# A scan beside a fused feed-forward: one y visit per chunk, and one scan operation between w and gT of each step

## The chip, the cores and the metric

The kernel runs on one core of a Trainium2 chip. The metric is the device time of one execution in microseconds (us); lower is better. All data are fp32.

## The reference

A Mamba-2 scan (4 sequences, 8 heads, 768 positions, head dimension 32, state dimension 16) is followed by a feed-forward block with the gate h cos h. In chunks, with `L` the running products of the decays `a`:

```python
M = CB * L                                  # CB = C B^T inside a chunk, causal
y_intra = M @ x
y_inter = (C @ state) * decay_to_i
y = y_intra + y_inter
state = decay_full * state + sum_j(B x * decay_from_j)
...
h = x @ w_in                                # x: y as 3072 rows of 256
g = h * cos(h)
out = g @ w_out                             # 256 -> 2048 -> 256
```

## The kernel before

The scan goes in 6 chunks (c = 0 to 5) of 128 positions. The feed-forward of one chunk, 4 x 128 = 512 rows, takes 16 *steps* (NF = 16), so there are 96 steps n. All engines follow one order written out by hand: the loop over n at the end. The scan of chunk c (c >= 1) is put into the steps of chunk c-1 and, before the change, the first steps of its own; chunk 0's scan stands ahead of the loop. "Place p of a chunk" is step 16(c-1) + p, for the scan of chunk c.

One step n issues, in this order:

- `first(n)`: TensorE computes hp = w_in^T y for 256 of the features and half of the rows (4 matmuls, 8 records, L512). ScalarE rounds it to k (L516), VectorE forms w = hp/2pi - k (L518).
- `gate(n)`: ScalarE takes the sine in place (L523). In steps 0 to 14 a `join` may follow, which assembles fp32 weights from their parts (VectorE L207 and L209, POOL L217).
- `gated(n)`: VectorE forms gT = hp * w (L528). From step 16 on, `differ(n)` follows on POOL: three products in a row that form gd from gT (L553, L555, L556).
- `second(n - 2)`: TensorE adds into o with gT and gd of two steps earlier. For chunk 0 that is 4 matmuls (L571); for the others `seven`, a scheme of 7 products (14 records, L609), in the order 1, 2, 6, 7, 5, 4, 3. Products 1 and 2 need gT, product 6 needs L555's output, product 7 is the first into the upper of o's two PSUM banks. After each eighth step the sums come out: ps is copied by ScalarE (L618) and VectorE (L619), then POOL makes four sums (L624), then DMAs on the SP queue. That is issued at steps 9 and 1 of a chunk's 16 (n = 25, 33, 41, ...). `differ_w`, two POOL products at a time (L547), stands in steps 14, 15, 17 and 19.

The scan of a chunk has these parts:

- `decays` (halves): VectorE's running product lam, 128 x 512, two for each sequence b (L344). After the second half, POOL forms sc (`weigh`, L327), and SP gets the load of that sequence's row `arow` for the next chunk.
- `reaches`: two running products of 128 for a pair of sequences u (L335); after them SP gets the load `along`.
- `turn2` (tp, L405): four transposes, copies bT and cT on ScalarE, rT on VectorE (L413).
- `intra2` (g, L422) one step later, and `masked`: m = g * lam, two VectorE operations per sequence (L435), the pair's first sequence in the g step, its second one a step later.
- `finish2` three steps after turn2: y of the pair, from the carried state (L447, tiles of 32 x 64 of the array) and from m (L454, tiles of 128 x 32), copied to yT by ScalarE (L459); then the chunk's sums s_ps (L471) and `carry`, two VectorE `whole` operations (L487) and a POOL product (L491).

For pair 0 of chunk c turn2 stands at place 11, for pair 1 at place 19 (`TURN`); the halves stand in the four steps ahead of each (chunk 1's first pair: steps 4, 6, 8, 9). In a step, masked, finish2, halves and reaches come after `second`.

PSUM has two hp buffers, so hp of step n+2 waits until gT of step n has read its own; two o banks; and two pair buffers ("scan") that tp, g, y and s_ps take in turn. m has two buffers.

Of the kernel before, what the change touches and what calls it, by code (L numbers as in the profile page):

```python
# [8 lines left out]
FP32 = mybir.dt.float32  # L9
# [16 lines left out]
def kernel(  # L26
# [62 lines left out]
    def pair(name):  # L89

        return psum.tile([P, 2, 4 * P], FP32, tag="scan", bufs=2, name=name)
# [109 lines left out]
    def join(which, i):  # L201

        parts = held.pop((which, i), ())
        for e, (high, bits, last) in enumerate(parts):
            V.tensor_scalar(out=bits, in0=bits, scalar1=3, scalar2=0x3FFFFFFF,  # L207
                            op0=ALU.logical_shift_left, op1=ALU.bitwise_and)
            V.scalar_tensor_tensor(out=bits, in0=high, scalar=0xC0000000, in1=bits,  # L209
                                   op0=ALU.bitwise_and, op1=ALU.bitwise_or)  # L210
            dst = kept(which, i)
            if len(parts) > 1:
                dst = dst[:, :, e * P:(e + 1) * P]
            else:
                bits, last = (ap.rearrange("p (k f) -> p k f", k=dst.shape[1])
                              for ap in (bits, last))
            G.tensor_tensor(out=dst.bitcast(U32), in0=bits, in1=last, op=ALU.add)  # L217
# [16 lines left out]
    unit = const.tile([P, HH, P], FP32, name="unit")  # L234
    G.tensor_copy(out=unit, in_=ident.unsqueeze(1).to_broadcast([P, HH, P]))

    unit0 = const.tile([P, H, W], FP32, name="unit0")
    for t in range(2):
        ts = slice(t * W, (t + 1) * W)
        V.tensor_copy(out=unit0[ts], in_=ident[ts, ts].unsqueeze(1).to_broadcast([W, H, W]))  # L240
# [30 lines left out]
                    axis=mybir.AxisListType.XY, op=ALU.add)  # L271


    a0s = const.tile([P, 2, H, W], FP32, name="a0s")
    halves = a0z.rearrange("p (t i) -> p t i", t=2)
    for h in range(HH):
        ACT.activation(a0s[:, :, h], halves, AF.Copy, scale=mine[:, h:h + 1])
    for t in range(2):
        G.tensor_tensor(out=a0s[:, t, HH:H], in0=halves[:, t:t + 1].to_broadcast([P, HH, W]),
                        in1=mine[:, HH:H].unsqueeze(2).to_broadcast([P, HH, W]), op=ALU.mult)  # L280
    tos = const.tile([P, H, W], FP32, name="tos")
    G.tensor_tensor(out=tos, in0=to.unsqueeze(1).to_broadcast([P, H, W]),
                    in1=mine.unsqueeze(2).to_broadcast([P, H, W]), op=ALU.mult)

# [83 lines left out]
    def intra(b):  # L368
        bT, cT = part[0, b]
        g = [pair("g") for _ in range(2)]  # L370
        for q in range(4):
            r = slice(32 * q, 32 * q + 32)
            PE.matmul(g[q // 2][:, q % 2, 0:2 * P], lhsT=bT[r],
                      rhs=cT[r].rearrange("p t (s i) -> p s t i", s=2), start=True, stop=True)
        l = lam.pop((0, b))
        m = scan.tile([P, 2, H, W], FP32, tag="m", name="m")
        for q in range(2):
            of = [t[:, :, q * HH:(q + 1) * HH].rearrange("p s (k t) i -> p k s (t i)", k=2)
                  for t in (m, l)]
            V.tensor_tensor(out=of[0], in0=g[q][:, :, 0:2 * P].rearrange(  # L380
                "p k (s i) -> p k s i", s=2), in1=of[1], op=ALU.mult)
        part[0, b] = m
# [16 lines left out]
    def turn2(c, u):  # L399
        bc = raw[c][0]  # L400

        tp = pair("tp")[:, 0].rearrange("p (s k i) -> p s k i", s=2, k=2)
        for s in range(2):
            for k in range(2):
                PE.transpose(tp[:, s, k],  # L405
                             bc[:, k, heads(2 * u + s)].rearrange("p h n -> p (h n)"), ident)
        bT = scan.tile([P, 2, P], FP32, tag="bT2", bufs=1, name="bT2")
        ACT.copy(out=bT, in_=tp[:, :, 0])
        cT = scan.tile([P, 2, 2, P], FP32, tag="cT2", bufs=1, name="cT2")
        for t in range(2):  # L410
            ACT.activation(cT[:, :, t], tp[:, :, 1], AF.Copy, scale=slot[:, t:t + 1])
        rT = scan.tile([P, 2, P], FP32, tag="rT", bufs=1, name="rT")
        V.tensor_tensor(out=rT, in0=tp[:, :, 1], in1=reach[c, u], op=ALU.mult)  # L413
        part[c, u] = [bT, cT, rT]

# [10 lines left out]
    def masked(c, b):  # L426

        u, s = divmod(b, 2)
        g, ms = part[c, u][0:2]
        l = lam.pop((c, b))  # L430
        m = scan.tile([P, H, P], FP32, tag="m", name="m")
        for q in range(2):
            of = [t[:, q * HH:(q + 1) * HH].rearrange("p (k t) i -> p k (t i)", k=2)
                  for t in (m, l)]
            V.tensor_tensor(out=of[0], in0=g[q][:, :, s * 2 * P:(s + 1) * 2 * P], in1=of[1],  # L435
                            op=ALU.mult)
        ms.append(m)

    def finish2(c, u):
        (_, ms, rT), xr = part.pop((c, u)), raw[c][1]  # L440
        y = pair("y")


        for s in range(2):
            for q in range(4):
                r, p = slice(32 * q, 32 * q + 32), 64 * (q % 2)
                PE.matmul(y[p:p + 64, q // 2, s * P:(s + 1) * P],  # L447
                          lhsT=state[c - 1, u][r, s].rearrange("p t d -> p (t d)"),
                          rhs=rT[r, s], start=(s == 0), stop=False, tile_position=(32 * q, p),
                          skip_group_check=True)  # L450
        for s in range(2):
            for h in range(H):
                q, t = h % 4, h // 4
                PE.matmul(y[32 * q:32 * q + 32, t, s * P:(s + 1) * P], lhsT=xr[:, 2 * u + s, h],  # L454
                          rhs=ms[s][:, h], start=False, stop=True, tile_position=(0, 32 * q),
                          skip_group_check=True)
        if u == 0:
            yT[c] = two.tile([P, 2, TB], FP32, tag="yT", name="yT")
        ACT.copy(out=yT[c][:, :, 2 * u * P:(2 * u + 2) * P], in_=y[:, :, 0:2 * P])  # L459
        if c < NC - 1:  # L460
            s_ps = pair("s_ps")[:, 0, 0:4 * D].rearrange("p (s d) -> p s d", s=2)
            for s in range(2):
                sum_up(c, 2 * u + s, s_ps[:, s])
            carry(c, u, s_ps)

    def sum_up(c, b, s_ps):

        xr, sc = raw[c][1], scaled.pop((c, b))
        for q in range(4):
            two_ = slice(2 * q, 2 * q + 2)  # L470
            PE.matmul(s_ps[32 * q:32 * q + 32], lhsT=sc[:, two_].rearrange("p h n -> p (h n)"),  # L471
                      rhs=xr[:, b, two_].rearrange("p h d -> p (h d)"), start=True, stop=True,
                      tile_position=(0, 32 * q), skip_group_check=True)
# [210 lines left out]
    for dst, src in ((a_cut, cut), (a_all, la)):  # L684
# [13 lines left out]
                 NF + 1: [(0, hind), (1, hind)], NF + 3: [(2, hind), (3, hind)]}  # L698


    TURN = (NF - 5, NF + 3)

    halves_of = {u: [(t - 4 + i, 2 * u + i // 2, i % 2) for i in range(4)]
                 for u, t in enumerate(TURN)}
    ahead = {1: {0: [(4, 0, 0), (6, 0, 1), (8, 1, 0), (9, 1, 1)]}}

    sums = {}

# [18 lines left out]

    def pairs(n):

        at = [(1 + (n - t) // NF, u) for u, t in enumerate(TURN) if (n - t) % NF == 0]  # L730
        return [(c, u) for c, u in at if 0 < c < NC]

    def halves_at(n):
        return [(c, b, t) for c in range(1, NC) for u in range(2)
                for m, b, t in ahead.get(c, {}).get(u, halves_of[u]) if m + (c - 1) * NF == n]

    EARLY = 3
    rest_of_loads()
    for n in range(NC * NF + LAG):
        c, f = divmod(n, NF)  # L740
        early = n < EARLY
        if n < NC * NF:
            if f == 0 and c > 0:
                load(c + 2)
            first(n)
            if n == 0:
                first_scan()
            for at in pairs(n):
                turn2(*at)
            rests = [grade(*piece[m], later=True)  # L750
                     for m in ((n,) if early else ()) + ((n + 1,) if n >= EARLY - 1 else ())
                     if m in piece]
            gate(n)
            for rest in rests:
                if rest:
                    rest()
            if not early and n in piece:
                join(*piece[n])
            gated(n)
            if early and n in piece:  # L760
                join(*piece[n])
            if n in (1, 2):
                carry(0, n - 1, sums[n - 1])
        for i, js in differ_at.get(n, ()):
            differ_w(i, js)
        if n >= LAG:
            second(n - LAG)
        for c, u in pairs(n - 1):
            intra2(c, u)
            masked(c, 2 * u)  # L770
        for c, u in pairs(n - 2):
            masked(c, 2 * u + 1)
        for c, u in pairs(n - 3):
            finish2(c, u)
            if u == 1:
                raw.pop(c)
        for c, b, t in halves_at(n):
            decays(c, b, t)
            if t == 1:
                load_a(c + 1, (b,))  # L780
        for c, u in pairs(n + 1):
            for b in (2 * u, 2 * u + 1):
                reaches(c, b)
                load_along(c + 1, (b,))
# [30 lines left out]
```

## Time and profile before

| what | value |
|---|---|
| median of 8 runs | 386.26 us (385.68 to 387.13) |
| profiled execution | 387.09 us, its span 385.3 us |
| TensorE matmul / weight load busy | 98% / 86% |
| VectorE, POOL, ScalarE busy | 69%, 64%, 45% |
| hp (L512): matmul records | 768, 184.4 us busy |
| o (L609, four kinds of row): matmul records | 1106, 176.1 us busy |
| scan lam (L344) | 40 of 1393 ns |
| granted TensorE clock | 1.000 |

The profile is of one execution. The span runs from the first to the last instruction; all times in its views count from the span's start. PE is TensorE, PEld its weight loads, DVE VectorE, ACT ScalarE, POOL GpSimd, SPq the DMA queue of SyncE. A row of the timeline gives the start, the duration, engine, line, operation, output and inputs; what stands in brackets is idle time ahead of it and what ended that. A row of the windows gives a stretch, its length, and for PE, PEld, DVE, ACT and POOL the busy time with the number of instructions, then the granted clock and the DMA's share and rate. A row of the waits gives the total time, the number of times and the longest.

### The profile page before, as it was taken

How to read it: one execution, taken by the hardware profiler on the slowest of the kernel's cores; microseconds unless marked ns; L12 is line 12 of the kernel's file. 1: busy time of each engine (PE TensorE's matmuls, PEld its weight loads, DVE VectorE, ACT ScalarE, POOL GpSimd, SP SyncE). 2: the span in 40 equal slices, each digit the busy share in tenths (PEclk: the TensorE clock that was granted, in tenths of full speed). 3: DMA queues.
4: the chain of work that ended last, by engine and by line, in shares of the span. 5: the costliest groups of instructions: out<-in, count | busy, mean ns of one | idle time of the engine just before them, and what ended most of it. 6: DMA issues, size and time to landing. Idle time of an engine off the chain costs nothing.

```text
span 385.3 us, 7726 instructions
## 1 busy us (share of the span) xinstructions
PE 378.7 (98%) x2982; PEld 331.2 (86%) x2982; DVE 265.9 (69%) x395; ACT 172.9 (45%) x303; POOL 245.8 (64%) x366
## 2 busy tenths in 40 slices
PE   8999999999999999999999999999999999999996
PEld 3478887888899899899899899899989989989995
DVE  7879999678758658657657757756765865863443
ACT  3777566434334334335334434434433433434441
POOL 4857675468759548648748837855955855853751
PEclk9999999999999999999999999999999999999999
DMA  7999899985001951301791301301210000010001
GB/s 91 274 253 267 229 239 126 165 95 156 0 2 57 151 54 57 96 2 54 126 81 55 97 2 54 91 9 41 68 45 1 19 10 2 2 27 3 6 23 27
DMA packets 106371, 30.42 MB, mean 79 GB/s; under 512 B 75520, under 2 KB 102240, under 8 KB 106336
## 3 DMA queue, kind: packets, MB, share of 16 engines
q1 hardware_dynamic: 106176, 29.81, 39.0%
q8 instruction: 23, 0.38, 0.4%
q10 hardware_dynamic: 160, 0.13, 0.1%
q14 instruction: 12, 0.10, 0.1%
HBM read 26.59 MB, written 3.34 MB: 78 GB/s over the span
## 4 chain that ended last, share of the span: by engine, by line
PE 78%; DVE 7%; POOL 4%; SPq 4%; ACT 3%; issue 2%; DMA 1%; POOLq 0%; ACTq 0%; DVEq 0%
PE hp L512 34%; PE o L609 30%; SPq L119 3%; PE g L422 3%; PE y L454 3%; DVE lam L344 2%; DVE w L518 2%; PE y L447 2%; PE o L571 1%; ACT w L523 1%; DVE gT L528 1%; PE warm L101 1%; DVE mag L209 1%; PE a_ps L298 1%; POOL gd L553 1%
## 5 line engine op out<-in xcount | busy, mean ns | idle before, releaser
L512 PE MATMUL hp<-yT,w_in 128*128 128x256 f32 x768 | 184.4, 383 | 0.7 <-POOL w_in L217 0.3
L512 PEld LDWEIGHTS hp<-yT,w_in 128*128 128x128 f32 x768 | 139.2, 190 | 22.7 <-issue 4.5
L553 POOL TENSOR_TENSOR gd<-gT 128x256 f32<-128x256 f32 x79 | 72.0, 912 | 89.1 <-DVE gT L528 85.9
L528 DVE TENSOR_TENSOR gT<-hp,w 128x512 f32<-128x512 f32 x96 | 66.3, 690 | 69.9 <-ACT w L523 60.1
L523 ACT ACTIVATE w<-w,quarter 128x512 f32<-128x512 f32 x96 | 69.3, 722 | 97.3 <-DVE w L518 97.3
L516 ACT ACTIVATE k<-hp 128x512 int32<-128x512 f32 x96 | 57.0, 594 | 90.8 <-PE hp L512 90.8
L518 DVE SCALAR_TENSOR_TENSOR w<-hp,k 128x512 f32<-128x512 f32 x96 | 65.3, 680 | 36.7 <-ACT k L516 36.5
L609 PE MATMUL o<-words,gd 128*128 128x128 f32 x474 | 67.0, 277 | 0.6 <-POOL gd L555 0.6
L609 PEld LDWEIGHTS o<-words,gd 128*128 128x128 f32 x474 | 59.3, 192 | 2.4 <-POOL gd L555 2.2
L344 DVE TENSOR_TENSOR_SCAN lam<-arow,unit 128x512 f32<-128x512 f32 x40 | 55.7, 1393 | 0.0
L609 PEld LDWEIGHTS o<-w_out,gT 128*128 128x128 f32 x316 | 46.9, 191 | 3.6
L609 PE MATMUL o<-w_out,gT 128*128 128x128 f32 x316 | 48.0, 274 | 0.0
L555 POOL TENSOR_TENSOR gd<-gT,gd 128x128 f32<-128x128 f32 x79 | 43.3, 548 | 6.2
L556 POOL TENSOR_TENSOR gd<-gT,gd 128x128 f32<-128x128 f32 x79 | 36.1, 457 | 6.2
L571 PE MATMUL o<-w_out,gT 128*128 128x256 f32 x128 | 30.3, 380 | 0.4 <-POOL w_out L217 0.4
L609 PE MATMUL o<-w_out,gd 128*128 128x128 f32 x158 | 30.6, 275 | 0.0
L609 PE MATMUL o<-words,gT 128*128 128x128 f32 x158 | 30.5, 275 | 0.0
L571 PEld LDWEIGHTS o<-w_out,gT 128*128 128x128 f32 x128 | 24.2, 190 | 4.0 <-POOL w_out L217 0.8
L435 DVE TENSOR_TENSOR m<-g,lam 128x512 f32<-128x512 f32 x40 | 25.5, 680 | 0.0
L624 POOL TENSOR_TENSOR sum<-ps,sum 128x256 f32<-128x256 f32 (+1 forms) x27 | 24.2, 908 | 1.4
L609 PEld LDWEIGHTS o<-words,gT 128*128 128x128 f32 x158 | 24.0, 192 | 0.0
L609 PEld LDWEIGHTS o<-w_out,gd 128*128 128x128 f32 x158 | 24.0, 192 | 0.0
(91 smaller groups left out, 294.3 us busy)
## 6 DMA issues: line engine op xcount, KB each, us to landing
arow<-a_cut SPq DMA_DIRECT2D x20, 512.0 KB
words<-in_moe_w_in_dram SPq DMA_DIRECT2D x8, 512.0 KB
words<-in_moe_w_out_dram SPq DMA_DIRECT2D x8, 512.0 KB
out_dram<-sum SPq DMA_DIRECT2D x18, 128.0 KB
xr<-in_x_dram SPq DMA_DIRECT2D x4, 512.0 KB
along<-a_all SPq DMA_DIRECT2D x20, 64.0 KB
xr<-in_x_dram SPq DMA_DIRECT2D x8, 128.0 KB
bc<-in_B_dram SPq DMA_DIRECT2D x4, 256.0 KB
```

What stands on the lines that cost most here:

```text
L344: V.tensor_tensor_scan(out=lam[c, b][:, hs].rearrange("p h i -> p (h i)"), data0=rows_.rearrange("p h i -> p (h i)"), data1=unit.rearrange ...
L435: V.tensor_tensor(out=of[0], in0=g[q][:, :, s * 2 * P:(s + 1) * 2 * P], in1=of[1], op=ALU.mult)
L512: PE.matmul(to_[:, e], lhsT=w_in[:, k, fs], rhs=y[:, k, u], start=(k == 0), stop=(k == KT - 1), skip_group_check=True)
L516: ACT.activation(k, hp[n], AF.Copy, bias=0.25, scale=INV_2PI)
L518: V.scalar_tensor_tensor(out=w, in0=hp[n], scalar=INV_2PI, in1=k, op0=ALU.mult, op1=ALU.subtract)
L523: ACT.activation(cos, cos, AF.Sin, bias=quarter, scale=TWO_PI)
L528: V.tensor_tensor(out=gT[n], in0=hp.pop(n), in1=cos, op=ALU.mult)
L553: G.tensor_tensor(out=d[:, 0:2], in0=g[:, 1:2].to_broadcast([P, 2, P]), in1=g[:, 3::-3], op=ALU.subtract)
L555: G.tensor_tensor(out=d[:, 2], in0=g[:, 0], in1=d[:, 0], op=ALU.subtract)
L556: G.tensor_tensor(out=d[:, 3], in0=g[:, 2], in1=d[:, 2], op=ALU.subtract)
L571: PE.matmul(o[c, u][:, t], lhsT=g[:, 2 * e + t], rhs=w_out[:, 2 * j + e], start=(j == e == t == 0), stop=(j == NJ - 1 and e == 1), skip_gr ...
L609: PE.matmul(at[q], lhsT=a_[q], rhs=w[q], start=(j == 0 and q in starts), stop=(j == NJ - 1), skip_group_check=True)
```

## The change

- `finish2` takes several pairs. For chunks 2 to 5 it runs once, at place 14, for both: all state products, all m products (y fills both banks of its pair buffer), then the copies to yT and the sums of all four sequences, then both carries. turn2 of the pairs stands at places 7 and 11. Chunk 1 keeps two visits, at steps 13 and 21, with turn2 at 10 and 18.
- Halves stand one per step: places -1 to 6 for chunks 3 to 5; chunk 1 in steps 4, 5, 7, 8 and 14 to 17, chunk 2 in steps 18, 19, 21 to 24, 26 and 27.
- From step 16 on, one operation of the scan, a pair of masked products or a half (with its sc), is issued ahead of `gated`, hence between w and gT on VectorE and ahead of differ on POOL. In steps 0 to 15 all of them come right after `gated`.
- m has four buffers, which unit0, tos and a0s of the beginning share; rT has two.

```diff
-    def finish2(c, u):
-        (_, ms, rT), xr = part.pop((c, u)), raw[c][1]
+    def finish2(c, us):
+        xr = raw[c][1]
+        parts = [(2 * u + s, part[c, u][1][s], part[c, u][2][:, s]) for u in us for s in range(2)]
         y = pair("y")
-        for s in range(2):
+        for i, (b, _, rT) in enumerate(parts):
             for q in range(4):
                 r, p = slice(32 * q, 32 * q + 32), 64 * (q % 2)
...
-        if u == 0:
-            yT[c] = two.tile([P, 2, TB], FP32, tag="yT", name="yT")
-        ACT.copy(out=yT[c][:, :, 2 * u * P:(2 * u + 2) * P], in_=y[:, :, 0:2 * P])
+        s_ps = pair("s_ps")[:, 0].rearrange("p (u s d) -> p u s d", u=2, s=2)
+        for i, u in enumerate(us):
+            del part[c, u]
+            if u == 0:
+                yT[c] = two.tile([P, 2, TB], FP32, tag="yT", name="yT")
+            ACT.copy(out=yT[c][:, :, 2 * u * P:(2 * u + 2) * P],
+                     in_=y[:, :, 2 * i * P:(2 * i + 2) * P])
+            for s in range(2 if c < NC - 1 else 0):
+                sum_up(c, 2 * u + s, s_ps[:, u, s, 0:2 * D])
         if c < NC - 1:
-            s_ps = pair("s_ps")[:, 0, 0:4 * D].rearrange("p (s d) -> p s d", s=2)
-            for s in range(2):
-                sum_up(c, 2 * u + s, s_ps[:, s])
-            carry(c, u, s_ps)
+            for u in us:
+                carry(c, u, s_ps[:, u, :, 0:2 * D])
...
-    TURN = (NF - 5, NF + 3)
-    halves_of = {u: [(t - 4 + i, 2 * u + i // 2, i % 2) for i in range(4)]
-                 for u, t in enumerate(TURN)}
-    ahead = {1: {0: [(4, 0, 0), (6, 0, 1), (8, 1, 0), (9, 1, 1)]}}
+    late = [((0,), {0: 10}, [(4, 0, 0), (5, 0, 1), (7, 1, 0), (8, 1, 1)], 13),
+            ((1,), {1: NF + 2}, [(NF - 2 + i, 2 + i // 2, i % 2) for i in range(4)], NF + 5)]
+    at_once = (0, 1), {0: 7, 1: 11}, 14
+    halves_of = {2: [(2, 0, 0), (3, 0, 1), (5, 1, 0), (6, 1, 1), (7, 2, 0), (8, 2, 1), (10, 3, 0),
+                     (11, 3, 1)]}
+    each = [(i - 1, i // 2, i % 2) for i in range(2 * NB)]
+    plan = [(c, NF * (c - 1), *v) for c in range(1, NC) for v in (
+        late if c == 1 else [(*at_once[:2], halves_of.get(c, each), at_once[2])])]
...
+            behind = [lambda at=at: halved(*at) for at in halves_at(n)]
+            behind = [lambda at=(c, 2 * u + 1): masked(*at) for c, u in pairs(n - 2)] + behind
+            if n not in piece and behind:
+                behind.pop(0)()
             gated(n)
+            for do in behind:
+                do()
...
-        for c, u in pairs(n - 2):
-            masked(c, 2 * u + 1)
-        for c, u in pairs(n - 3):
-            finish2(c, u)
-            if u == 1:
+        for c, us in ends(n):
+            finish2(c, us)
+            if 1 in us:
                 raw.pop(c)
-        for c, b, t in halves_at(n):
-            decays(c, b, t)
-            if t == 1:
-                load_a(c + 1, (b,))
```

`halved` is `decays` with the load of `arow` behind the second half; `ends(n)` gives the visits that end in step n; `piece` holds steps 0 to 15.

More of the change, by code (lines that the diff above doesn't have):

```diff
@@ L235 @@
     G.tensor_copy(out=unit, in_=ident.unsqueeze(1).to_broadcast([P, HH, P]))
-    unit0 = const.tile([P, H, W], FP32, name="unit0")
+    both = scan.tile([P, 2, H, W], FP32, tag="m", bufs=4, name="both")
+    unit0, tos = both[:, 0], both[:, 1]
     for t in range(2):
@@ L271 @@
                     axis=mybir.AxisListType.XY, op=ALU.add)
-    a0s = const.tile([P, 2, H, W], FP32, name="a0s")
+    a0s = scan.tile([P, 2, H, W], FP32, tag="m", bufs=4, name="a0s")
     halves = a0z.rearrange("p (t i) -> p t i", t=2)
@@ L280 @@
                         in1=mine[:, HH:H].unsqueeze(2).to_broadcast([P, HH, W]), op=ALU.mult)
-    tos = const.tile([P, H, W], FP32, name="tos")
     G.tensor_tensor(out=tos, in0=to.unsqueeze(1).to_broadcast([P, H, W]),
@@ L375, in intra @@
         l = lam.pop((0, b))
-        m = scan.tile([P, 2, H, W], FP32, tag="m", name="m")
+        m = scan.tile([P, 2, H, W], FP32, tag="m", bufs=4, name="m")
         for q in range(2):
@@ L411, in turn2 @@
             ACT.activation(cT[:, :, t], tp[:, :, 1], AF.Copy, scale=slot[:, t:t + 1])
-        rT = scan.tile([P, 2, P], FP32, tag="rT", bufs=1, name="rT")
+        rT = scan.tile([P, 2, P], FP32, tag="rT", name="rT")
         V.tensor_tensor(out=rT, in0=tp[:, :, 1], in1=reach[c, u], op=ALU.mult)
@@ L430, in masked @@
         l = lam.pop((c, b))
-        m = scan.tile([P, H, P], FP32, tag="m", name="m")
+        m = scan.tile([P, H, P], FP32, tag="m", bufs=4, name="m")
         for q in range(2):
@@ L437, in masked @@
         ms.append(m)
-    def finish2(c, u):
-        (_, ms, rT), xr = part.pop((c, u)), raw[c][1]
+    def finish2(c, us):
+        xr = raw[c][1]
+        parts = [(2 * u + s, part[c, u][1][s], part[c, u][2][:, s]) for u in us for s in range(2)]
         y = pair("y")
-        for s in range(2):
+        for i, (b, _, rT) in enumerate(parts):
             for q in range(4):
                 r, p = slice(32 * q, 32 * q + 32), 64 * (q % 2)
-                PE.matmul(y[p:p + 64, q // 2, s * P:(s + 1) * P],
-                          lhsT=state[c - 1, u][r, s].rearrange("p t d -> p (t d)"),
-                          rhs=rT[r, s], start=(s == 0), stop=False, tile_position=(32 * q, p),
+                PE.matmul(y[p:p + 64, q // 2, i * P:(i + 1) * P],
+                          lhsT=state[c - 1, b // 2][r, b % 2].rearrange("p t d -> p (t d)"),
+                          rhs=rT[r], start=(i == 0), stop=False, tile_position=(32 * q, p),
@@ L450, in finish2 @@
                           skip_group_check=True)
-        for s in range(2):
+        for i, (b, m, _) in enumerate(parts):
             for h in range(H):
                 q, t = h % 4, h // 4
-                PE.matmul(y[32 * q:32 * q + 32, t, s * P:(s + 1) * P], lhsT=xr[:, 2 * u + s, h],
-                          rhs=ms[s][:, h], start=False, stop=True, tile_position=(0, 32 * q),
+                PE.matmul(y[32 * q:32 * q + 32, t, i * P:(i + 1) * P], lhsT=xr[:, b, h],
+                          rhs=m[:, h], start=False, stop=True, tile_position=(0, 32 * q),
@@ L460, in finish2 @@
         if c < NC - 1:
-            s_ps = pair("s_ps")[:, 0, 0:4 * D].rearrange("p (s d) -> p s d", s=2)
-            for s in range(2):
-                sum_up(c, 2 * u + s, s_ps[:, s])
-            carry(c, u, s_ps)
+            for u in us:
+                carry(c, u, s_ps[:, u, :, 0:2 * D])
     def sum_up(c, b, s_ps):
@@ L728, in pairs, with halved, ends @@
     def pairs(n):
-        at = [(1 + (n - t) // NF, u) for u, t in enumerate(TURN) if (n - t) % NF == 0]
-        return [(c, u) for c, u in at if 0 < c < NC]
+        return [(c, u) for c, at, _, turn_at, _, _ in plan for u in turn_at
+                if at + turn_at[u] == n]
     def halves_at(n):
-        return [(c, b, t) for c in range(1, NC) for u in range(2)
-                for m, b, t in ahead.get(c, {}).get(u, halves_of[u]) if m + (c - 1) * NF == n]
+        return [(c, *h) for c, at, _, _, halves_of, _ in plan for m, *h in halves_of if at + m == n]
+    def halved(c, b, t):
+        decays(c, b, t)
+        if t == 1:
+            load_a(c + 1, (b,))
+    def ends(n):
+        return [(c, us) for c, at, us, _, _, end in plan if at + end == n]
     EARLY = 3
```

## Prediction, made before the changed kernel ran

> **What bounds the kernel now.** The page comes first: busy time by engine, then the chain that ended last.
>
> ```profile
> PE 378.7 (98%) x2982; PEld 331.2 (86%) x2982; DVE 265.9 (69%) x395; ACT 172.9 (45%) x303; POOL 245.8 (64%) x366
> ...
> PE 78%; DVE 7%; POOL 4%; SPq 4%; ACT 3%; issue 2%; DMA 1%; POOLq 0%; ACTq 0%; DVEq 0%
> ```
>
> TensorE is busy for 98% of the span at a granted clock of 1.00, so only what shortens its own work, or a wait of its own, counts. Next the windows, one per step, from one hp start to the next (steps 65 to 71: an hp, an o, and a visit to the scan in some):
>
> ```profile
> 264.50:267.79 3.29, 3.29 (x24) 3.08 (x23) 2.43 (x4) 1.32 (x2) 2.42 (x3) 1.00 0.00 0
> 267.79:271.08 3.29, 3.29 (x24) 3.08 (x23) 2.43 (x4) 1.69 (x3) 2.78 (x5) 1.00 0.53 159
> 271.08:274.81 3.73, 3.73 (x28) 3.47 (x27) 2.87 (x5) 2.32 (x5) 3.49 (x5) 1.00 0.02 4
> 274.81:279.52 4.71, 4.71 (x41) 3.86 (x39) 3.40 (x6) 1.93 (x3) 4.17 (x8) 1.00 0.45 119
> 279.52:282.91 3.39, 3.39 (x26) 3.18 (x23) 2.56 (x4) 0.60 (x1) 2.15 (x5) 1.00 0.38 108
> 282.91:288.12 5.21, 5.21 (x88) 4.62 (x86) 3.19 (x6) 2.12 (x4) 1.80 (x4) 1.00 0.02 3
> 288.12:291.51 3.39, 3.39 (x29) 3.18 (x23) 1.14 (x3) 1.10 (x2) 1.84 (x4) 1.00 0.00 0
> ```
>
> A plain step is 3.29 us. Above that, one pair's visit costs 0.44 (tp), 1.42 (g), 0.10 (the hp after g), 1.92 (y and sums) and 0.10 (the hp after y). Waits of TensorE's weight loads after 100 us (total, times, longest):
>
> ```profile
> PEld hp L512 <- issue: 3.1, 10, 0.3
> PEld y L454 <- issue: 1.5, 9, 0.2
> PEld o L609 <- POOL gd L555: 1.5, 8, 0.3
> PEld o L609 <- DVE ps L619: 0.2, 1, 0.2
> ```
>
> The first two are changes of tile shape. The third is a real wait, in each of the eight g steps after 100 us: there o takes 1.90 where o before y takes 1.655, so 0.25 each (0.32 in step 52), 2.06 in all. Step 20 has the same wait at 0.83. The fourth, in step 50, is 0.28. The timeline of steps 57 to 59 (hp of 57 starts at 234.20, w at 236.82) says why:
>
> ```profile
> 238.37 0.69 DVE L528 TENSOR_TENSOR gT<-hp,w 128x512 f32<-128x512 f32 x1 [0.86 <-ACT w L523]
> 238.45 0.42 POOL L327 TENSOR_TENSOR sc<-bc,lam 128x128 f32<-128x128 f32 x1
> 238.98 0.68 DVE L619 COPY ps<-o 128x512 f32<-128x512 f32 x1
> 239.21 0.73 POOL L553 TENSOR_TENSOR gd<-gT 128x256 f32<-128x256 f32 x1 [0.34 <-DVE gT L528]
> ...
> 239.58 1.44 DVE L344 TENSOR_TENSOR_SCAN lam<-arow,unit 128x512 f32<-128x512 f32 x1
> ...
> 240.01 1.25 POOL L555 TENSOR_TENSOR gd<-gT,gd 128x128 f32<-128x128 f32 x1
> ...
> 242.57 2.87 POOL L624 TENSOR_TENSOR sum<-ps,sum 128x256 f32<-128x256 f32 x3
> ```
>
> Scan and POOL exclude each other. L555 takes 0.46 alone and 1.25 beside the scan; L553 0.73 and 1.51; the scan 1.21 alone, 1.44 when L553 was first; the last three sums 1.96 at 362.55 where no scan runs, and 2.87 here. So POOL is late with differ(58): its L555 ends at 246.77, and TensorE's third product of step 60 wanted it at 246.68 (hp start 244.51 + 1.73 + 0.44).
>
> **The merged visit.** In step 62's visit (the timeline in narrow windows) the matmuls start four at a time. From o to y 0.205 passes instead of 0.111. The state products start at 255.99 and 256.15, then every 0.11; 0.22 passes to the first m product, then 0.13, then 0.11; the sums go every 0.056; the hp after is 0.10 longer. One visit costs 0.09 + 0.60 + 0.90 + 0.34 + 0.10 = 2.02. A second pair in the same visit adds only its groups, 4 x 0.11 + 8 x 0.109 + 4 x 0.056 = 1.53. So 0.49 is saved in each of chunks 2 to 5 (chunk 5 has no sums and saves the same shape changes): **-1.96**. TensorE's own work, nothing hides it. The two yT copies and four `whole` operations stand before an hp that starts after them; the second pair's `whole` waits for POOL's state product (0.40), still before w of the next step, 2.6 after hp's start. Four m buffers and two rT buffers (0.68 and 0.41 an operation) are costed at nothing: those matmuls come at least a step after them. If that cover fails, one visit loses at most such an operation. unit0, tos and a0s now share m's buffers; all three are read before the third and fourth m of chunk 0 are written: nothing.
>
> **The scan between w and gT.** Times from the hp start of a step: w at 2.62, scan at 3.23. The sine ends by 4.1, the scan lets the next operation go 1.13 after its start, so gT is at 4.36, not 4.17; if a POOL product holds the scan up, as late as 4.8. A masked pair there (2 x 0.60) puts gT at 4.43. hp two steps later needs gT by 5.75 (6.58 less the 0.83 between gT and hp at 60.12 and 60.95), so a plain step loses nothing. Three things change elsewhere:
>
> - *ps.* At places 1 and 9 of a chunk, ps is queued behind gT. It ends at 239.66; TensorE's load for the upper bank starts at 239.78 and follows it by 0.05, so there is 0.07 of slack (step 50, gT 0.35 late: 0.28 lost). Masked steps 25, 41, 57, 73: 0.26 - 0.07 = 0.19 each, **+0.76**. Scan steps 33, 49, 65: between 0.12 and 0.56; I take 0.30, nearest the unheld scan, **+0.90**.
> - *POOL after the sums, places 1 to 4 of chunks 3 to 5* (waits in steps 36, 52, 68). Scans now stand in every step, and sc of place 2 is queued ahead of differ. From 5.20 (gT + 0.84) POOL has three differ products (0.81, 0.54, 0.54 from start to start), four sums (3 x 0.81, 0.54), sc (0.50), L553 and L555 (0.81, 0.46): 6.63. Two scans hold it 0.78 each: 13.4. TensorE wants that L555 at 12.16 (three plain steps, 9.87, the wait of at least 0.12 at ps, and 1.73 + 0.44 into its step). Another way: late by 0.15 now, + 0.50 for sc, + 0.44 since the tp step is gone from between, + 0.19 for gT: 1.28. I take 1.3, three times, **+3.9**; the bounds are 0 (no hold) and 1.6 (two holds of 0.98).
> - *The same after step 25*: scan, two reaches and scan fall on the sums; L555 at 13.3 against 12.67: **+0.8** in step 28 (0 to 1.0). At place 9 of the later chunks no scan is near and L555 ends by 12.0 against 12.67: no wait.
>
> So the waits named above go, **-2.06 - 0.83 - 0.28**. Step 20's goes because reaches and scans of steps 18 and 19 no longer fall on the two differ_w products (3.42 where 2 x 1.27 is their unheld length).
>
> One rule of the Trainium skill (SBUF — State Buffer, Who interferes with whom) bears on this: a VectorE operation with two SBUF inputs and a GpSimd one that reads SBUF exclude each other for the whole instruction, whoever starts first. It speaks against the change, since a sum that started first now holds the scan and gT behind it. With whole holds of 1.21 in place of 0.78 the three waits would add 3 x 0.86 = 2.6 more (390.3); the rows have POOL going again 1.0 after an unheld scan's start (scan at 232.40, L553's 1.51 ending at 234.13, less its own 0.73), and I go by the rows.
>
> **Chunk 1 and the start.** In steps to 15 the scan remains behind gT. A VectorE step with join and scan takes 4.1 to 4.7 (w at 42.50 to 46.91), one without 2.5; TensorE's is 3.45. The scans of chunk 1 move from steps 4, 6, 8, 9 to 4, 5, 7, 8: w of step 6 at 44.1 instead of 42.5, so hp of step 8 no sooner than 46.7 against 46.16, 0.57 lost; now steps 5, 10 and 11 lose 0.5 in that way. With the later steps I take **+0.2** (-0.4 to +1.2). On SP, arow and along of chunk 2 are issued one to ten steps sooner, but behind the loads that SP ends at 63, and are needed from step 18 (85 us): nothing; one late landing would cost up to the 3.4 that arow took at 36.61.
>
> **Sum**: -1.96 - 2.06 - 0.83 - 0.28 + 0.76 + 0.90 + 3.9 + 0.8 + 0.2 = **+1.43**. The profiled execution took 387.09 (span 385.3 and 1.8 around it) and would take 388.5; it lies 0.83 above the median of 386.26, which becomes **387.7**.
>
> **Rivals.**
> - *POOL keeps up*: the new waits at steps 28, 36, 52, 68 don't come. For it: POOL is 36% idle, and 6.63 from 5.20 without a hold is 11.8, before 12.16. Against: every scan beside a POOL product stretched it by 0.78. Sum -3.3: **383.0**. Chance 0.28.
> - *Half holds, and a start that costs its 1.2*: half of the 4.7 goes (one scan of the two finds POOL between products) and 1.0 is added in chunk 1: 1.43 - 2.35 + 1.0, no change, **386.3** (385.4 to 387.0). Chance 0.18.
> - *gT itself becomes the limit* (slower by more): scan held by POOL beyond the 1.39 between 4.36 and 5.75, so that hp two steps later waits. For it: sums follow each other within 0.08. Against: the scan got in after one sum at 243.06. At 0.25 in each of 32 scan steps, +8: **394**. Chance 0.05.
> - *It doesn't do what it says*: up to step 15 nothing is moved between; that is in the sum.
>
> The forecast has the remaining 0.49. A measurement can tell about 0.2% (0.8 us) from no change. Faster 0.30 (the first rival and an edge of the second), same 0.17, slower 0.53. The likeliest case alone spans 386.9 to 390.0; with the first rival's centre the range is 383.0 to 390.0, leaving out its lower half and the last rival.
>
> **What would show it.** y visits of chunks 2 to 4 of 2.02 + 1.53 = 3.55 above two plain steps (3.1 in chunk 5). o before g at 1.66 in place of 1.90, except step 28. In steps 36, 52 and 68, an o of 2.9 with its wait on gd L555; in 34, 50 and 66 an o some 0.3 longer, waiting on ps. L553 back at 0.73 in most steps. No such o, and the first rival holds; hp waiting on gT after 100 us is the third; steps 4 to 12 more than 1.2 longer would break the start's estimate.

## The result, and the profile after

The changed kernel takes 388.26 us (median of 13 runs, 387.23 to 388.65) beside 386.81 of the kernel before: a ratio of 1.0038, 95% interval 1.0029 to 1.0047. It is slower by 1.5 us. Its profiled execution took 387.95 with a span of 386.2; that span is only 0.9 above the one of before, because the first hp started at 18.56 and not at 19.21. From the first hp to the end of TensorE's last matmul, the steps take 363.95 in place of 362.42, which is the 1.5 of the medians.

The page after, busy time and the chain that ended last:

```profile
PE 376.7 (98%) x2982; PEld 331.2 (86%) x2982; DVE 264.9 (69%) x395; ACT 173.1 (45%) x303; POOL 238.6 (62%) x366
...
PE 80%; POOL 8%; DVE 5%; issue 3%; ACT 2%; POOLq 0%; ACTq 0%
```

TensorE's busy time has fallen by 2.0 and still the steps are longer: the gain is in its own work, the loss in waits. POOL's share of the chain has doubled, though POOL is busy for less time. The windows of steps 33 to 36 (places 1 to 4 of chunk 3) show a step in which PE is idle for 1.25 (5.07 less 3.82); before, no step after 100 us had more than 0.06 of that:

```profile
145.88:149.17 3.29, 3.29 (x25) 3.08 (x23) 2.65 (x5) 1.32 (x2) 1.82 (x4) 1.00 0.23 69
149.17:152.58 3.41, 3.41 (x25) 3.16 (x24) 3.15 (x6) 1.75 (x4) 2.70 (x5) 1.00 0.29 87
152.58:155.87 3.29, 3.29 (x25) 3.08 (x24) 2.29 (x4) 1.25 (x2) 3.13 (x4) 1.00 0.00 0
155.87:160.94 5.07, 3.82 (x25) 3.23 (x24) 4.35 (x6) 2.04 (x3) 4.91 (x7) 1.00 0.34 88
```

Beside a plain step of 3.29, step 34 is 0.12 too long (the wait for ps) and step 36 is 1.78 too long. The merged visits, by contrast, save time. Here is chunk 2's, in step 30, with the step after it:

```profile
132.45:139.19 6.74, 6.74 (x152) 6.15 (x150) 3.19 (x6) 2.35 (x4) 3.22 (x6) 1.00 1.50 112
139.19:142.59 3.40, 3.40 (x30) 3.19 (x23) 1.62 (x6) 1.37 (x3) 0.87 (x3) 1.00 0.18 17
```

That is 3.56 above two plain steps, for two pairs; before, one pair cost 2.02. The waits of TensorE's weight loads after 100 us:

```profile
PEld o L616 <- POOL gd L562: 3.1, 4, 1.1
PEld hp L519 <- issue: 2.9, 9, 0.3
PEld o L616 <- POOL gd L563: 1.0, 2, 0.5
PEld y L457 <- issue: 0.9, 5, 0.2
```

L562 and L563 are L555 and L556 of before, L560 is L553, L616 is L609, L631 is L624. The eight small waits on gd have given way to three large ones (steps 36, 52 and 68) and a small one (step 28), and twice TensorE waits again, on the third differ product. The timeline of steps 34 to 36 (hp of step 33 starts at 145.88) shows how:

```profile
151.07 0.73 POOL L560 TENSOR_TENSOR gd<-gT 128x256 f32<-128x256 f32 x1 [0.47 <-PE hp L519]
...
152.39 1.22 DVE L345 TENSOR_TENSOR_SCAN lam<-arow,unit 128x512 f32<-128x512 f32 x1
152.42 1.44 POOL L563 TENSOR_TENSOR gd<-gT,gd 128x128 f32<-128x128 f32 x1
...
154.62 2.86 POOL L631 TENSOR_TENSOR sum<-ps,sum 128x256 f32<-128x256 f32 x3
...
155.80 1.43 DVE L345 TENSOR_TENSOR_SCAN lam<-arow,unit 128x512 f32<-128x512 f32 x1
...
157.44 0.41 POOL L328 TENSOR_TENSOR sc<-bc,lam 128x128 f32<-128x128 f32 x1
...
157.81 0.73 POOL L560 TENSOR_TENSOR gd<-gT 128x256 f32<-128x256 f32 x1
158.62 0.46 POOL L562 TENSOR_TENSOR gd<-gT,gd 128x128 f32<-128x128 f32 x1
...
159.09 1.22 DVE L345 TENSOR_TENSOR_SCAN lam<-arow,unit 128x512 f32<-128x512 f32 x1
159.13 0.60 PE L616 MATMUL o<-words,gd 128*128 128x128 f32 x3 [0.92 <-POOL gd L562]
159.15 1.41 POOL L563 TENSOR_TENSOR gd<-gT,gd 128x128 f32<-128x128 f32 x1
```

The scan at 152.39 gets in 0.03 ahead of L563, which then takes 1.44 (alone 0.46). The scan at 155.80 waits for a sum and then holds the last one. sc stands ahead of differ(34). L562 ends at 159.08, 13.20 after the hp of step 33; TensorE would have taken it at 12.16. L563 meets the next scan, at 159.09, and is late as well. But for this second wait it is what the forecast said; the runs below test it.

### The profile page after: what moved, and what is told of

Read it like the earlier page. It is cut to its first block, busy times and chain, and to the rows that moved or that the text cites. A ratio compares the mean times of both kernels' runs of the same rounds, so it can differ in the third digit from the quotient of the medians.

```text
span 386.2 us, 7716 instructions
## 1 busy us (share of the span) xinstructions
PE 376.7 (98%) x2982; PEld 331.2 (86%) x2982; DVE 264.9 (69%) x395; ACT 173.1 (45%) x303; POOL 238.6 (62%) x366
## 4 chain that ended last, share of the span: by engine, by line
PE 80%; POOL 8%; DVE 5%; issue 3%; ACT 2%; POOLq 0%; ACTq 0%
PE hp L519 36%; PE o L616 29%; PE g L423 3%; POOL sum L631 3%; PE o L578 3%; PE y L457 2%; POOL gd L560 2%; PE y L450 1%; DVE mag L209 1%; POOL words L554 1%; PE warm L101 1%; DVE w L525 1%; DVE gT L535 1%; PE tp L406 1%; PE a_ps L299 1%
## 5 line engine op out<-in xcount | busy, mean ns | idle before, releaser
L560 POOL TENSOR_TENSOR gd<-gT 128x256 f32<-128x256 f32 x79 | 60.4, 764 | 86.7 <-DVE gT L535 57.0
L535 DVE TENSOR_TENSOR gT<-hp,w 128x512 f32<-128x512 f32 x96 | 65.1, 679 | 32.3 <-ACT w L530 30.5
L616 PE MATMUL o<-words,gd 128*128 128x128 f32 x474 | 67.5, 278 | 2.5 <-POOL gd L562 2.4
L616 PEld LDWEIGHTS o<-words,gd 128*128 128x128 f32 x474 | 59.8, 192 | 4.1 <-POOL gd L562 3.4
L563 POOL TENSOR_TENSOR gd<-gT,gd 128x128 f32<-128x128 f32 x79 | 48.8, 618 | 6.2
L616 PEld LDWEIGHTS o<-w_out,gT 128*128 128x128 f32 x316 | 46.9, 191 | 3.5
L616 PE MATMUL o<-w_out,gT 128*128 128x128 f32 x316 | 48.0, 274 | 0.0
L562 POOL TENSOR_TENSOR gd<-gT,gd 128x128 f32<-128x128 f32 x79 | 37.8, 479 | 6.2
L616 PE MATMUL o<-w_out,gd 128*128 128x128 f32 x158 | 30.8, 276 | 0.6 <-POOL gd L563 0.6
L616 PE MATMUL o<-words,gT 128*128 128x128 f32 x158 | 30.5, 275 | 0.0
L616 PEld LDWEIGHTS o<-w_out,gd 128*128 128x128 f32 x158 | 24.0, 192 | 1.0 <-POOL gd L563 1.0
L616 PEld LDWEIGHTS o<-words,gT 128*128 128x128 f32 x158 | 24.0, 192 | 0.0
L631 POOL TENSOR_TENSOR sum<-ps,sum 128x256 f32<-128x256 f32 (+1 forms) x27 | 20.0, 754 | 1.4
```

Of the source, the lines that this page charges most:

```text
L535: V.tensor_tensor(out=gT[n], in0=hp.pop(n), in1=cos, op=ALU.mult)
L560: G.tensor_tensor(out=d[:, 0:2], in0=g[:, 1:2].to_broadcast([P, 2, P]), in1=g[:, 3::-3], op=ALU.subtract)
L562: G.tensor_tensor(out=d[:, 2], in0=g[:, 0], in1=d[:, 0], op=ALU.subtract)
L563: G.tensor_tensor(out=d[:, 3], in0=g[:, 2], in1=d[:, 2], op=ALU.subtract)
L616: PE.matmul(at[q], lhsT=a_[q], rhs=w[q], start=(j == 0 and q in starts), stop=(j == NJ - 1), skip_group_check=True)
L631: G.tensor_tensor(out=dst, in0=a_, in1=b_.to_broadcast([P, dst.shape[1], P]), op=ALU.add)
```

## The experiments

There are three theories. **T**: the waits of steps 36, 52 and 68 come of POOL, which scans hold up in the very steps in which it makes the four sums; sc ahead of differ is a part of it, and the merged visit is a gain. **R1**: the loss comes of gT being late behind a VectorE operation. **R2**: the long visit itself does harm.

**e1_behind: nothing between w and gT.** The steps stay, the operations go behind `second` again.

```diff
-            behind = [lambda at=at: halved(*at) for at in halves_at(n)]
-            behind = [lambda at=(c, 2 * u + 1): masked(*at) for c, u in pairs(n - 2)] + behind
-            if n not in piece and behind:
-                behind.pop(0)()
             gated(n)
-            for do in behind:
-                do()
...
+        for c, u in pairs(n - 2):
+            masked(c, 2 * u + 1)
+        for at in halves_at(n):
+            halved(*at)
         for c, us in ends(n):
```

> Undone: the place between w and gT. All scan operations stand behind second again (masked products and halves at the end of a step), while the halves stay one per step and the merged visit stays. Theory T (POOL loses the waits of steps 36, 52 and 68 because halves stand in the very steps in which the four sums run, wherever in the step they are): the seven waits for ps go (-1.05), but the waits of steps 36 and 52 stay at 1.6 to 1.8 and that of step 68 grows to about the same, since L562 of place 2 still ends near 13.6 against 12.04; the waits of steps 20 and 28 may come back. Time about 388.3 (387.3 to 389.2). Rival R1 (the loss comes of gT being late behind a scan): all the new waits go, 382 to 383. Rival R2 (the long merged visit starves or delays other engines): unchanged at 388.3 but with waits next to steps 30, 46, 62 and 78.

Measured: 385.87, ratio to before 0.9994 (0.9982 to 1.0006). All three theories missed. R1's 382 to 383 did not come: steps 36, 52 and 68 still wait, 0.83 each. But T had 1.6 to 1.8; I had forgotten that sc comes behind differ in this kernel too. Nor is gT early throughout: that of step 33 starts 4.10 after its hp, but those of 34 and 35 start at 4.89 and 4.97 (4.36 and 4.58 in the changed kernel), since the scan behind ps now stands ahead of their w. So e1 does not rule R1 out. The ps waits went, as T said (-1.05), and so did those of steps 18, 20 and 28; new ones came: 1.16 in step 21 (y waits for m) and 0.83 in step 26 (ps behind a late gT). Each of the three waits on gd has two parts: TensorE's load waits 0.30 for L562 and then 0.38 for L563. So e1 alone doesn't tell the placement from the order of sc; e4 moves the order alone.

**e4_sc_later: sc behind differ.** The scan stays between w and gT.

```diff
-        if t == 0 or c == NC - 1:
-            return
-        weigh(c, b)
+        if t == 1 and c < NC - 1:
+            late_sc.append((c, b))
...
             for do in behind:
                 do()
+            while late_sc:
+                weigh(*late_sc.pop(0))
```

> One thing moved: sc (POOL, L328) is issued behind differ of its step and no longer ahead of it; the scan stays between w and gT. Theory T: L562 and L563 of place 2 come 0.50 sooner in chunks 3 and 4, L563 then ends before the scan of place 4, so the waits of steps 36 and 52 fall from 1.78 to the 0.81 that step 68 shows, where chunk 5 has no sc: 388.3 - 1.9 = 386.3. R1 and R2: no change, 388.3.

Measured: 386.14, ratio 0.9999 (0.9988 to 1.0009). Steps 36, 52 and 68 wait 0.82, 0.82 and 0.82, and but for 0.06 more in step 20 no other step moved. The whole wait is now for the second differ product, which is L563 in this kernel's numbering and L562 in that of the changed one (after 100 us):

```profile
PEld o L617 <- POOL gd L563: 2.2, 3, 0.7
```

That is what T expected; R1 and R2 had no change. The one product of 0.41 costs 0.96 a time, since with it the third differ product falls behind the next scan; here it starts 0.31 ahead of that scan. That the total agrees with e1's 0.83 is a coincidence, as the two waits are made up of different parts.

**e2_clear: no half in places 1 to 3.**

```diff
-    each = [(i - 1, i // 2, i % 2) for i in range(2 * NB)]
+    each = [(-1, 0, 0), (0, 0, 1), (4, 1, 0), (5, 1, 1), (6, 2, 0), (7, 2, 1), (8, 3, 0),
+            (12, 3, 1)]
```

> One thing moved: in chunks 3 to 5 the halves stand at places -1, 0, 4, 5, 6, 7, 8 and 12 rather than -1 to 6, so none runs in places 1 to 3, where the sums are made; they still stand between w and gT. Theory T: the waits on gd of steps 36, 52 and 68 (4.37) and the three scan waits on ps in steps 34, 50 and 66 (0.37) go and nothing else changes: 388.3 - 4.7 = 383.6. R1 (late gT): only the ps waits go, since gT is as late in the other steps: 387.9. R2 (merged visit): unchanged, 388.3.

Measured: 383.44, ratio 0.9926 (0.9910 to 0.9942). All six waits, on gd and on ps, are gone (4.77 in sum), and no other step changed by more than 0.02: ps at places 9 still costs 0.17 each, steps 18, 20 and 28 cost 0.35, 0.20 and 0.21. The four sums are busy for 2.64, where it was 3.55, and L563 of differ(33) takes 0.46 in place of 1.44. With no scan there, gT is early as well in these steps (4.10 to 4.17), so e2 alone does not part T from R1; e6 does.

**e6_no_hold: the same time on VectorE, without the scan.** This leaves out the running products at places 2 and 3 of chunks 3 to 5 and puts copies from PSUM in their place.

```diff
         rows_ = arow[c, b][:, hs]
+        if c > 2 and (b, t) in ((1, 1), (2, 0)):
+            for e in range(2):
+                V.tensor_copy(out=lam[c, b][:, hs].rearrange("p h i -> p (h i)"),
+                              in_=hp[NF * (c - 1) + b + 1])
+            if t == 1 and c < NC - 1:
+                weigh(c, b)
+            return
```

> The changed kernel, but in chunks 3 to 5 the halves at places 2 and 3 are not running products: two copies of hp from PSUM (one SBUF operand, 2 x 0.60 us on VectorE) fill that part of lam in their stead. That leaves out the decays of one sequence's second half and the next one's first half of the heads. gT stays as late behind them as behind a scan or a little later (4.43 after hp against 4.36), but nothing holds POOL. Theory T (POOL held by the scans): the four sums take 2.8 us, not 3.7, and the waits of steps 36, 52 and 68 go altogether: 388.3 - 4.4 = 383.9. R1 (gT late behind a VectorE operation): the waits stay, 388.3 or more. R2: 388.3.

Measured: 383.63, ratio 0.9916 (0.9901 to 0.9931). Its timeline, in the same two steps of chunk 4 (hp of step 49 starts at 206.33):

```profile
212.85 1.41 DVE L347 COPY lam<-hp 128x512 f32<-128x512 f32 x2
212.87 0.46 POOL L570 TENSOR_TENSOR gd<-gT,gd 128x128 f32<-128x128 f32 x1
...
214.09 1.95 POOL L638 TENSOR_TENSOR sum<-ps,sum 128x256 f32<-128x256 f32 x3
214.17 0.68 DVE L542 TENSOR_TENSOR gT<-hp,w 128x512 f32<-128x512 f32 x1
...
216.00 0.42 POOL L328 TENSOR_TENSOR sc<-bc,lam 128x128 f32<-128x128 f32 x1
...
217.19 0.46 POOL L569 TENSOR_TENSOR gd<-gT,gd 128x128 f32<-128x128 f32 x1
```

L570 (L563) starts 0.02 behind the copy, as it did behind the scan, and takes 0.46 and not 1.44; the last three sums take 1.95 in place of 2.86. gT of step 50 (7.84 after the hp of step 49) is later than behind a scan (7.65 in the changed kernel), sc is still ahead of differ, and L569 (L562) ends at 11.32 after the hp of step 49: no wait in 36, 52 or 68, and no other step changed by more than 0.02. So neither gT's time nor sc alone makes the wait; the scan's hold on POOL does. That is T, and R1 is out.

**e3_two_visits: the merge undone.**

```diff
-        late if c == 1 else [(*at_once[:2], halves_of.get(c, each), at_once[2])])]
+        late if c == 1 else [((0,), {0: 7}, halves_of.get(c, each), 10), ((1,), {1: 11}, [], 14)])]
```

> Undone: the merged visit. Chunks 2 to 5 have a y visit for pair 0 at place 10 and one for pair 1 at place 14, everything else as in the changed kernel. Theory T: each of the four chunks pays the changes of tile shape again, 0.49 each, and TensorE's waits stay where they are: 388.3 + 1.97 = 390.2. R2 (the long visit costs): faster than 388.3 by what it costs. R1 is silent on it.

Measured: 389.39, ratio 1.0087 (1.0070 to 1.0104), where the changed kernel had 1.0038. The time is 0.8 below the 390.2 expected; 0.5 of that lies in the kernel before, which took 386.32 beside these runs and 386.81 beside the changed kernel's. In the profiles the visits take 1.97 more in sum, as expected, and other waits 0.3 less (0.23 of it in step 28, whose wait went with a visit in step 26). R2 falls: the merge is a gain.

**e5_best: put together.** e2, with three more edits: at places 9 the masked pair stands behind ps; chunk 2's last halves in steps 27 and 28; chunk 1's first pair on the steps it had before.

```diff
+            sums_out = n >= NF + 9 and n % NJ == 1
-            if n not in piece and behind:
+            if n not in piece and behind and not sums_out:
                 behind.pop(0)()
             gated(n)
-            for do in behind:
+            for do in () if sums_out else behind:
                 do()
...
             second(n - LAG)
+        if n < NC * NF and sums_out:
+            for do in behind:
+                do()
...
-    late = [((0,), {0: 10}, [(4, 0, 0), (5, 0, 1), (7, 1, 0), (8, 1, 1)], 13),
+    late = [((0,), {0: 11}, [(4, 0, 0), (6, 0, 1), (8, 1, 0), (9, 1, 1)], 14),
...
-    halves_of = {2: [(2, 0, 0), (3, 0, 1), (5, 1, 0), (6, 1, 1), (7, 2, 0), (8, 2, 1), (10, 3, 0),
-                     (11, 3, 1)]}
+    halves_of = {2: [(2, 0, 0), (3, 0, 1), (5, 1, 0), (6, 1, 1), (7, 2, 0), (8, 2, 1), (11, 3, 0),
+                     (12, 3, 1)]}
```

> A version put together from the findings: halves of chunks 3 to 5 away from places 1 to 3 (as in e2); at places 9 the masked pair behind ps, no longer between w and gT; chunk 2's last two halves a step later and two steps later (27, 28), clear of its sums; chunk 1's first pair back on steps 4, 6, 8, 9 with turn2 at 11 and its visit at 14. Theory T: 383.4 of e2, less 4 x 0.17 (ps), less 0.21 (step 28), less 0.46 (steps 4 to 11): 382.1, all of TensorE's waits after step 20 gone. R1 and R2 say no more than that it isn't slower than e2.

Measured: 381.28, ratio 0.9862 (0.9848 to 0.9876): faster than both kernels. The waits of its weight loads after 100 us are none on gd, gT or ps; what is left stands where the tile shape changes:

```profile
PEld hp L519 <- issue: 1.5, 5, 0.3
PEld hp L519 <- DVE lam L345: 1.3, 4, 0.3
PEld y L457 <- issue: 0.9, 5, 0.2
```

No o from step 18 on is longer than its plain 1.56 or, ahead of g and y, 1.655. (The second row is the hp after g in steps 29, 45, 61 and 77. These steps are 0.10 above plain ones, as in both kernels, so I take it for the shape change, with a scan's end near by.) It was 0.8 faster than expected; 0.57 of that are the waits of steps 18 and 20, which went too.

**e7_best_behind: e5 with nothing between w and gT.** The edit is that of e1 on e5.

> The version e5 with one thing undone: nothing stands between w and gT any more, all masked pairs and halves come behind second, on the same steps as in e5. Theory T: the place between w and gT is worth nothing on the path where halves and sums don't meet; L553 beside a scan goes to 1.5 again, but POOL has the time. Within 0.3% of e5, 381.3 to 382.4; if a wait comes, it is at steps 20 to 22, where differ_w and the scans of chunk 2 meet (e1 had 1.16 in step 21). A theory in which the place between w and gT was the gain of the change: the eight waits of before come back, 383.3 or more.

Measured: 385.36, ratio 0.9977 (0.9966 to 0.9989), 4.1 above e5. Here my theory was wrong: I had said that the place between w and gT is worth nothing where halves and sums don't meet. But the waits aren't those of before either; none is on gd. After 60 us (a part of the list):

```profile
PEld o L616 <- ACT ps L625: 2.4, 4, 0.6
PEld hp L519 <- DVE w L525: 1.7, 5, 0.3
PEld o L616 <- DVE ps L626: 1.1, 4, 0.3
```

They are in steps 26, 42, 58 and 74, 0.82 each, and 0.80 stands in step 21. VectorE's timeline around step 57, whose hp starts at 235.18, tells why:

```profile
235.73 0.69 DVE L535 TENSOR_TENSOR gT<-hp,w 128x512 f32<-128x512 f32 x1 [0.86 <-ACT w L530]
236.34 1.28 DVE L436 TENSOR_TENSOR m<-g,lam 128x512 f32<-128x512 f32 x2
237.54 1.37 DVE L345 TENSOR_TENSOR_SCAN lam<-arow,unit 128x512 f32<-128x512 f32 x1
238.83 0.66 DVE L525 SCALAR_TENSOR_TENSOR w<-hp,k 128x512 f32<-128x512 f32 x1
```

At place 8 (step 56) the masked pair and a half follow one another behind gT, and w of step 57, wanted at 237.80, comes 1.03 late; gT and ps with it. Between w and gT the half fills the 0.86 in which VectorE otherwise waits for the sine. So the place is worth that much in this plan, and by VectorE's order, not POOL's.

## Why the prediction was right

It forecast slower, +1.4, and the steps grew by 1.53. Term by term, from the steps' lengths in the two profiles:

| term | forecast | measured |
|---|---|---|
| merged visits | -1.96 | -1.97 |
| waits of before that go | -3.17 | -3.17 |
| ps behind masked, 4 | +0.76 | +0.68 |
| ps behind a scan, 3 | +0.90 | +0.37 |
| POOL after the sums, steps 36, 52, 68 | +3.9 | +4.37 |
| step 28 | +0.8 | +0.23 |
| start (steps 3 to 17) | +0.2 | +0.46 |
| steps 18 and 20 | 0 | +0.57 |
| sum | +1.43 | +1.54 |

- *The merged visit* held to 0.01: the part of a visit that the merge saves lies where the tile shape changes, and it could be read off the starts of the groups of four matmuls (the five items of one visit add up to 2.03, a hundredth above the 2.02 that I wrote).
- *The main term* was right in mechanism (e2, e4, e6). That its size is near is partly luck, since it is a sum of unequal parts: 1.78, 1.78 and 0.81 where I had 1.3 three times, and two of them lie above the 1.6 that I called the bound. I missed that chunk 5 has no sc, and that a late L563 meets the next scan: in steps 36 and 52 TensorE's load waits 1.11 for L562 and then 0.52 for L563. Nor is 0.78 what every scan costs a product beside it: the two in question cost 0.98 (L563, 1.44 against 0.46) and 0.91 (the last three sums, 2.86 against 1.95).
- *ps behind a scan*: mis-sized. It cost 0.12 to 0.13 each, the lower bound, since POOL held the scan up by only 0.04 (in step 33 it was recorded for 1.25 against 1.21): L562 of the step before ended 0.17 into it, and L563 came behind it.
- *Step 28*: mis-sized; L562 ended at 12.83 after the hp of step 25 where I had 13.3, because the L560 ahead of it started 0.05 before the scan that I let it lose to.
- *The start* was 0.26 more. Step 7 lost 0.68, where I had 0.57, and step 8 lost 0.08; against that the step with tp (10 in place of 11) came out 0.23 shorter, and the 0.05 that step 10 lost before went.
- *Steps 18 and 20*: not seen. I had the wait of step 20 go altogether; it fell from 0.83 to 0.21, and step 18 got 0.36. Both are on gd L562. They are gone in e5, whose only edit to e2 ahead of them is the move of chunk 1's first pair, and they are gone in e1 too, where that pair stays and nothing stands between w and gT from step 16 on. So more than one thing removes them, and their cause stays open.
- *The sum is better than its terms, by luck*: 0.08, 0.53 and 0.57 too much (ps, step 28) against 0.47, 0.26 and 0.57 too little (the main term, the start, steps 18 and 20).

The whole-instruction rule of the Trainium skill (SBUF — State Buffer, Who interferes with whom) would have given 390.3. In the trace L563 of differ(33) was recorded for 1.44 from 152.42; less its own 0.46 it began at 153.40, 1.0 after the scan's start, while the scan's row is 1.22. The measurement decides for the rows: the main term came out 0.47 above the forecast, not 2.6. The same section states that a VectorE instruction with at most one SBUF input, outside its 2-port modes, does not contend with GpSimd. e6 agrees: beside its copies, whose input lies in PSUM, L563 took 0.46.

The rivals: "POOL keeps up" would have been right only in e2 and e6. Its 383.0 is what the change gives without that conflict (383.4). "gT itself becomes the limit" didn't come; after 100 us no row has an hp waiting on gT.

## What to carry to other kernels

Where two engines exclude each other, as the scan and POOL do here, spreading one's work evenly over all steps can be worse than bunching it: what counts is in which steps the other one has its backlog, and how late its next product may come. Add up that engine's queue from the wait backwards, holds included, against the time at which the consumer wants it; a small product (0.41) put ahead in that queue may cost twice its length. A gain in the bounding engine's own work (here 0.49 for each visit merged) can be kept if the rest of the change is taken apart: with the scans out of three steps of a chunk the change that cost 0.4% gives 0.7%, and with its other waits removed 1.4%. What a place in the order is worth depends on the plan around it: the place between w and gT is worth 4.1 in e5, and undoing it in the changed kernel (e1, which moves sc as well) gave a faster kernel.

## What the runs showed of the hardware that was not expected

- In these traces a POOL row's duration holds its wait for VectorE. L563 of 128 x 128 is recorded at 0.46 alone and at 1.41 to 1.44 when a scan began 0.03 to 0.06 ahead of it.
- The scan at 155.80 got in between two sums that otherwise follow each other within 0.08: the engine that waited came in when the other's current product ended, and the rest of the other's queue came behind it.
- The time ahead of the first hp differs from profile to profile: 19.21 and 18.56 in the two above, and 17.95 to 19.41 in the changed kernel and its seven variants, whose edits leave that part alone, while steps that no edit touched repeat within some hundredths. Spans of single profiles of this kernel should be compared from the first hp on.
